# A fourth weight buffer and later products in an attention and SwiGLU kernel

## The chip, the cores and the metric

The kernel runs on one core of a Trainium2 chip. The core has five engines that work side by side, each through its own queue of instructions in order: TensorE (PE in the profile, its weight loads apart as PEld), VectorE (DVE), ScalarE (ACT), GpSimd (POOL) and SyncE (SP, which here only issues transfers). They wait for each other through semaphores. Transfers between the main memory and the on-chip memory (SBUF) run beside them. Matrix products land in PSUM[...].

The metric is the device time of one execution in microseconds (us), as the median of a few runs.

## The reference

Attention comes first: 8 batches, 8 heads, 576 positions, head size 64. Of each row of scores only the 32 largest count. Its output, with the heads side by side, is the input of a feed-forward block with 4,608 tokens, width 512 and 1,536 inner channels.

```python
scores = scale * np.matmul(q, k.transpose(0, 1, 3, 2))
kth = np.partition(scores, -top_k, axis=-1)[..., -top_k:-top_k + 1]
scores = np.where(scores >= kth, scores, -1000000000.0)
attn = np.exp(scores - np.max(scores, axis=-1, keepdims=True))
attn = attn / (np.sum(attn, axis=-1, keepdims=True) + 1e-09)
x = np.matmul(attn, v)          # then (B,H,S,D) -> (B*S, H*D)
g = x @ w_gate
out = (g * (1.0 / (1.0 + np.exp(-g))) * (x @ w_val)) @ w_out
```

The inputs q, k and v and the output are float32. The three weight matrices arrive as float64.

## The kernel before, in words

**Units.** Attention is cut into units of one batch, 128 query rows (64 in the last tile of a batch) and two heads. The main loop (line 833) goes through them and holds several at once in different stages. For unit n, `scores` makes q times k on PE (line 310, line 296 for the short tile) and ACT copies the result to `sc` (lines 315, 301). `select` finds the 32 largest on DVE, with four rounds of MAX8 (line 330) and three of MATCH_REPLACE8 (line 334) per head. `shift` subtracts on POOL (line 345). `weigh` makes the exponentials on ACT (lines 357 and 362), and leaves their sum in `tot`. `normalize` takes the reciprocal on DVE (lines 373, 374) and scales e on POOL (line 380) or ACT (line 378). `turn` transposes e on PE into `etps` (line 394), and ACT copies it (line 395). `values` multiplies with v on PE (line 428), and ACT copies the product into `xT` (line 444), the transposed input of the feed-forward block.

**Feed-forward.** A block has 256 tokens. The first two are done in halves of 128 tokens and in the plain way by `feed_half` (products with w_gate and w_val, line 488; ACT evacuates them in lines 508 to 515, POOL multiplies in lines 511 and 516) and `out_half` (product with w_out into `o_ps`, line 540). From the third block on, `feed` does the work (lines 572 and 638), with a scheme for the last product that needs sums and differences of parts of w_out. It can start only when all six early jobs (four halves in, two halves out) are issued and all heads of the block are in `xT`.

**Rounding.** The weights arrive as float64, that is as pairs of 32-bit words, and the kernel rounds them to float32 by itself from the two words. They come in 36 pieces of 512 KB: 12 of w_gate, 12 of w_val, in turns of two, then 12 of w_out, one per 128 inner channels. `rounded` handles one: SP loads it into a buffer `w` (line 104), ACT makes three passes over it (lines 112, 114, 115), DVE shifts (line 119), POOL adds and multiplies (lines 120, 121), and line 121 writes the rounded piece to its place in `wg`, `wv` or `wo`. Line 121 is also the last reader of the buffer. Buffers of one tag are reused in turn, so the load of a piece waits until line 121 of the piece that had the buffer before. `weights` steps the pieces through three stages with lags, and counts in `ready` how many have been issued to the end. The later part of `weights` forms the sums and differences of w_out on POOL (lines 169, 177, 181, 185); its first three tiles `t` have the tag of the weight buffers too.

**Who decides the order.** The order on PE, DVE, ACT and POOL is the order in which the Python program issues instructions, since the end of the kernel ties each to the one before it on its engine. SP's order is left to the framework. A product is issued when `piece` finds a job that may go on: `feed_half` and `out_half` ask `sure(n)` before each product, and give the turn back when it says no. `sure` does not wait on the chip. It compares a counter while the program is written, so that a product is placed in PE's queue at a point where the rounding of its piece has already been issued. A credit of time per unit (`share`) limits how many products are put into one unit.

Of the kernel before, what the change touches and what calls it, by code (L numbers as in the profile page):

```python
# [10 lines left out]
FP32 = mybir.dt.float32  # L11
I32 = mybir.dt.int32
# [3 lines left out]
P = 128  # L16
# [5 lines left out]
WP = 256  # L22
# [3 lines left out]
def kernel(  # L26
# [39 lines left out]
    DM, DFF = w_gate.shape  # L66
# [5 lines left out]
    MC = DFF // P  # L72
    MS = MC // 2
# [11 lines left out]
    ffn = ctx.enter_context(tc.tile_pool(name="ffn", bufs=2))  # L85
# [14 lines left out]

    def rounded(src, dst):

        w = ffn.tile([P, 2, WP, 2], I32, tag="w", name="w", bufs=3)
        nc.sync.dma_start(
            w[:].rearrange("p c f t -> p c (f t)"), src.bitcast(I32)
        )
        yield
        low, high = w[:, :, :, 0], w[:, :, :, 1].bitcast(FP32)


        size = conv.tile([P, 2, WP], FP32, tag="size", name="size", bufs=3)
        nc.scalar.activation(size[:], high, AF.Abs, scale=2.0**-112)

        nc.scalar.mul(low, low.bitcast(U32), 2.0**-29)
        nc.scalar.sign(high, high)
        yield

        bits = size[:].bitcast(I32)
        nc.vector.tensor_single_scalar(bits, bits, 3, ALU.logical_shift_left)
        nc.gpsimd.tensor_tensor(bits, bits, low, ALU.add)  # L120
        nc.gpsimd.tensor_tensor(dst, size[:], high, ALU.mult)  # L121

    def weights():


        pieces = []
        for f in range(0, DFF, WP):
            for src, dst in ((w_gate, wg), (w_val, wv)):
                for c in range(0, KC, 2):
                    rows = src[c * P : (c + 2) * P, f : f + WP]  # L130
                    pieces.append((
                        rows.rearrange("(c p) f -> p c f", p=P), dst[:, c : c + 2, f : f + WP]
                    ))
        for c in range(MC):
            pieces.append((
                w_out[c * P : (c + 1) * P].rearrange("p (c f) -> p c f", c=2),
                wo[:, c].rearrange("p (c f) -> p c f", c=2),
            ))
        pieces = [rounded(*p) for p in pieces]
        step = [0] * len(pieces)  # L140

        def upto(i, k):

            while 0 <= i < len(pieces) and step[i] < k:
                next(pieces[i], None)
                step[i] += 1


        lags = (5, 2, 0)
        for n in range(2 * len(pieces) + 4):  # L150
            for k, lag in enumerate(lags):
                if (n - lag) % 2 == 0:
                    upto((n - lag) // 2, len(lags) - k)
            ready[0] = max((n - 5) // 2 + 1, 0)
            early[0] = lambda: upto(n // 2, 2)
            yield
        early[0] = lambda: None


        add, sub = ALU.add, ALU.subtract  # L160
        lo, hi = slice(0, DM // 2), slice(DM // 2, DM)
        room = []
        for _ in range(3):
            t = ffn.tile([P, 4, DM // 2], FP32, tag="w", name="t", bufs=3)
            room += [t[:, 0:2], t[:, 2:4]]
        for m in range(0, MQ, 2):
            mm, nn = slice(m, m + 2), slice(MQ + m, MQ + m + 2)
            t3 = room.pop()
            nc.gpsimd.tensor_tensor(t3, wo[:, nn, hi], wo[:, mm, hi], sub)
            T[7] += [t3[:, i, :] for i in range(2)]  # L170
            yield
        while not plain_done:
            yield
        for m in range(0, MQ, 2):
            mm, nn = slice(m, m + 2), slice(MQ + m, MQ + m + 2)
            t1 = wo[:, mm, hi]
            nc.gpsimd.tensor_tensor(t1, t1, wo[:, mm, lo], sub)
            T[5] += [wo[:, m + i, hi] for i in range(2)]
            yield
            t2 = room.pop()  # L180
            nc.gpsimd.tensor_tensor(t2, wo[:, nn, hi], t1, sub)
            T[6] += [t2[:, i, :] for i in range(2)]
            yield
            t4 = conv.tile([P, 2, DM // 2], FP32, tag="size", name="t4", bufs=3)
            nc.gpsimd.tensor_tensor(t4[:], wo[:, nn, lo], t2, sub)
            T[4] += [t4[:, i, :] for i in range(2)]
            yield
        T[1] += [wo[:, m, lo] for m in range(MQ)]
        T[2] += [wo[:, MQ + m, lo] for m in range(MQ)]
        T[3] += [wo[:, MQ + m, hi] for m in range(MQ)]  # L190
        yield

    ready = [0]
    early = [lambda: None]
    plain_done = []
    T = {i: [] for i in range(1, 8)}
    weight = weights()

    def rounding(n):
# [7 lines left out]

    def sure(n):

        return ready[0] >= min(n + 1, 4 * MS + MC)  # L210

    pairs = [(b, hp) for b in range(B) for hp in range(NHP)]
    raw, preps = {}, {}
# [259 lines left out]
    def feed_half(kb, t):  # L473
# [7 lines left out]
        def product(w, g, then):  # L481
            ps = ps_f.tile([P, 4, P], FP32, tag="f", name="f")
            for i in range(4):
                m = 4 * g + i
                while not sure(4 * (m // 2) + (2 if w is wg else 4)):
                    yield None
                for kc in range(KC):
                    nc.tensor.matmul(  # L488
                        ps[:, i, :],
                        w[:, kc, m * P : (m + 1) * P],  # L490
                        x[:, kc, cols],
                        start=(kc == 0),
                        stop=(kc == KC - 1),
                    )
                if i == 3:
                    on_act.append(lambda: then(ps))
                if i % 2 == 1:
                    yield 1
# [25 lines left out]
    def out_half(t):  # L524
# [7 lines left out]
        while not sure(4 * MS + 2):  # L532
            yield None
# [3 lines left out]
        for m in range(MC):  # L537
            while not sure(4 * MS + m + 1):
                yield None
            nc.tensor.matmul(  # L540
                ps[:], hs[m // 4][:, m % 4, :], wo[:, m, :], start=(m == 0), stop=(m == MC - 1)
            )
            if m == MC - 1:

                def finish():
                    nc.scalar.copy(o[:, t, :], ps[:])
                    store(o[:, t, :], t * P)

                on_act.append(finish)
                told.append(t)  # L550
                if t == 1:
                    plain_done.append(True)
            if m % 2 == 1:
                yield 1
# [389 lines left out]
```

## Time and profile before

| | |
|---|---|
| median of 3 runs | 1777.67 us (1777.34 to 1779.84) |
| the profiled execution, its own time | 1777.1 us |
| its span, first to last instruction | 1775.3 us |
| PE busy | 1683.9 us, 95% of the span |
| PEld busy (beside PE) | 1404.2 us, 79% |
| DVE busy | 1484.1 us, 84% |
| ACT busy | 1257.0 us, 71% |
| POOL busy | 798.9 us, 45% |
| granted TensorE clock, mean | 0.970 of full speed |
| loads of weight pieces, issue to landing, median | 3.5 to 3.7 us |
| moved by transfers | 59.73 MB, mean 34 GB/s |

The shares are means over stages that differ. The first feed-forward product starts at 86 us, the last weight piece is rounded at 197 us, the third block of tokens begins at 347 us, and attention's last transposes come at 1709 us; after them only feed-forward work is left. So the profile is read by stage. In a timeline each row gives the start, the length, the engine, the line of the kernel, the operation and, in brackets, the time for which the engine had been idle just before and what released it.

### The profile page before, as it was taken

The page shows a single profiled execution, that of the slowest core. Times are in us where ns is not written, and L with a number is a line of the kernel's source. Part 1 is how long each engine was busy: PE and PEld are TensorE (multiplying, and loading weights), DVE is VectorE, ACT ScalarE, POOL GpSimd, SP SyncE. Part 2 cuts the span into 40 slices and gives each one's busy share as a digit, 9 for nine tenths or more (in the row PEclk, how much of TensorE's full clock was granted, in tenths as well). Part 3 has the DMA queues.
Part 4 walks back from the last instruction along what each step waited for, and adds up shares of the span by engine and source line. Part 5 has one row for each costly group of instructions (what it writes and reads, how often), then busy time and mean ns, then how long its engine had stood idle before and what let it go on. Part 6 is the DMA issues. An engine that isn't in the chain of part 4 may idle for free.

```text
span 1775.3 us, 31791 instructions
## 1 busy us (share of the span) xinstructions
PE 1683.9 (95%) x11396; PEld 1404.2 (79%) x11396; DVE 1484.1 (84%) x3371; ACT 1257.0 (71%) x2869; POOL 798.9 (45%) x910
## 2 busy tenths in 40 slices
PE   4578999799999999999999999999999999999999
PEld 3477588688888878887888878888888888888887
DVE  6999699998898898997989978998988889898300
ACT  7788686777777677767777776767776777676531
POOL 4788545234353525352444425453335343535344
PEclk7689899899999999999999999999999999999999
DMA  7433030002100030001200021000300010000000
GB/s 197 127 106 96 20 81 9 12 2 58 39 1 13 2 81 15 13 1 35 62 13 1 13 60 37 1 13 2 94 1 13 1 44 27 13 1 13 1 13 12
DMA packets 109310, 59.73 MB, mean 34 GB/s; under 512 B 88544, under 2 KB 96992, under 8 KB 109152
## 3 DMA queue, kind: packets, MB, share of 16 engines
q1 hardware_dynamic: 108016, 57.37, 12.2%
q8 instruction: 90, 1.47, 0.4%
q14 instruction: 68, 0.56, 0.1%
q10 hardware_dynamic: 1136, 0.33, 0.1%
HBM read 48.23 MB, written 9.44 MB: 32 GB/s over the span
## 4 chain that ended last, share of the span: by engine, by line
PE 83%; ACT 7%; POOL 4%; DVE 4%; issue 2%; DMA 1%; SPq 0%; POOLq 0%; ACTq 0%
PE f L572 37%; PE av L428 10%; PE x_ps L638 9%; PE s L310 7%; PE y_ps L638 7%; PE etps L394 6%; PE f L488 3%; ACT e L362 2%; PE s L296 2%; DVE e L334 2%; DVE m L330 2%; PE kqps L265 1%; ACT e L357 1%; POOL wo L121 1%; POOL e L380 1%
## 5 line engine op out<-in xcount | busy, mean ns | idle before, releaser
L330 DVE MAX8 m<-e 128x8 f32<-128x576 f32 x864 | 615.5, 749 | 3.3
L334 DVE MATCH_REPLACE8 e<-m,e 128x576 f32<-128x576 f32 x576 | 424.1, 743 | 0.0
L572 PE MATMUL f<-xT,wg 128*128 128x256 f32 x1536 | 353.5, 381 | 0.0
L572 PE MATMUL f<-xT,wv 128*128 128x256 f32 x1536 | 353.1, 380 | 0.0
L572 PEld LDWEIGHTS f<-xT,wg 128*128 128x128 f32 x1536 | 286.8, 190 | 44.4 <-issue 7.9
L572 PEld LDWEIGHTS f<-xT,wv 128*128 128x128 f32 x1536 | 287.1, 190 | 43.4 <-issue 6.8
L608 POOL TENSOR_TENSOR h<-h,half_g 128x512 f32<-128x512 f32 x96 | 122.5, 1276 | 332.9 <-ACT h L607 324.9
L362 ACT ACTIVATE e<-e,bias 128x576 f32<-128x576 f32 x288 | 221.1, 775 | 34.6 <-POOL bias L345 31.5
L394 PE MATMUL etps<-ident,e 128*128 128x128 f32 (+1 forms) x1312 | 182.8, 281 | 42.9 <-POOL e L380 18.4
L357 ACT ACTIVATE e<-sc,m 128x576 f32<-128x576 f32 x288 | 211.2, 785 | 2.6 <-DVE m L330 2.6
L394 PEld LDWEIGHTS etps<-ident,e 128*128 128x128 f32 (+1 forms) x1312 | 154.7, 143 | 72.9 <-POOL e L380 23.4
L334 DVE MATCH_REPLACE8 e<-m,sc 128x576 f32<-128x576 f32 x288 | 212.0, 743 | 0.0
L330 DVE MAX8 m<-sc 128x8 f32<-128x576 f32 x288 | 203.4, 743 | 9.1 <-ACT sc L315 9.1
L613 POOL TENSOR_TENSOR h<-h,val 128x512 f32<-128x512 f32 x96 | 122.5, 1276 | 194.7 <-ACT val L612 170.9
L373 DVE TENSOR_SCALAR tot<-tot 128x1 f32<-128x1 f32 x288 | 37.2, 146 | 199.7 <-ACT e L362 199.6
L315 ACT ACTIVATE sc<-s 128x288 f32<-128x288 f32 x512 | 167.4, 414 | 49.4 <-PE s L310 49.0
L310 PE MATMUL s<-kqT 64*128 64x288 f32 x1024 | 173.3, 450 | 24.5 <-ACT et L395 11.1
L380 POOL TENSOR_TENSOR e<-e,tot 128x576 f32<-128x576 f32 x140 | 161.1, 1155 | 77.0 <-DVE tot L374 69.2
L395 ACT COPY et<-etps 128x512 f32<-128x512 f32 (+1 forms) x448 | 183.4, 489 | 13.5 <-PE etps L394 13.3
L428 PE MATMUL av<-et,v 128*64 128x128 f32 (+1 forms) x2560 | 161.4, 270 | 0.0
L310 PEld LDWEIGHTS s<-kqT 64*128 64x128 f32 x1024 | 96.0, 194 | 71.9 <-issue 22.9
L378 ACT ACTIVATE e<-e,tot 128x576 f32<-128x576 f32 x148 | 118.4, 800 | 42.8 <-DVE tot L374 42.6
(82 smaller groups left out, 2274.5 us busy)
## 6 DMA issues: line engine op xcount, KB each, us to landing
v<-in_v_dram SPq DMA_DIRECT2D x32, 256.0 KB, 3.1
kq_in<-in_k_dram SPq DMA_DIRECT2D x63, 128.0 KB, 2.8
kq_in<-in_q_dram SPq DMA_DIRECT2D x63, 128.0 KB, 3.1
w<-in_moe_w_gate_dram SPq DMA_DIRECT2D x12, 512.0 KB, 3.7
w<-in_moe_w_val_dram SPq DMA_DIRECT2D x12, 512.0 KB, 3.7
w<-in_moe_w_out_dram SPq DMA_DIRECT2D x12, 512.0 KB, 3.5
out_dram<-o SPq DMA_DIRECT2D x38, 128.0 KB, 2.4
out_dram<-o SPq DMA_DIRECT2D x16, 256.0 KB, 2.6
```

The lines of the kernel that those rows point to most:

```text
L310: nc.tensor.matmul(ps[:, 0:half], slab[d, q0 : q0 + P], slab[d, k0 : k0 + half])
L315: nc.scalar.mul(sc[:, i * half : (i + 1) * half], ps[:, 0:half], scale)
L330: nc.vector.max(m[:, t, 8 * r : 8 * r + 8], cur[:, hs])
L334: nc.vector.match_replace(e[:, hs], m[:, t, 8 * r : 8 * r + 8], cur[:, hs], LOWEST)
L357: nc.scalar.activation(e[:, hs], sc[:, hs], AF.Prelu, bias=m[:, t, TOP_K - 1 : TOP_K], scale=-1.0, alpha=SMALL,)
L362: nc.scalar.activation(e[:, hs], e[:, hs], AF.Exp, bias=bias[:, t : t + 1], scale=-1.0 / SMALL, accum_out=tot[:, t : t + 1],)
L380: nc.gpsimd.tensor_tensor(e[:, hs], e[:, hs], tot[:, t : t + 1].to_broadcast([P, S]), ALU.mult)
L394: nc.tensor.transpose(ps[0:kl, c * P : (c + 1) * P], e[:, k0 : k0 + kl], ident[:])
L395: nc.scalar.copy(et[0:kl, c0 : c0 + cn, :], ps[0:kl, 0 : cn * P].rearrange("p (c j) -> p c j", c=cn),)
L428: nc.tensor.matmul(av[d, i, 0:ql], weights_, moving, start=c == (0 if last else J), stop=c == (J if last else J - 1),)
L572: nc.tensor.matmul(ps[:, i, :], w[:, kc, m * P : (m + 1) * P], x[:, kc, :], start=(kc == 0), stop=(kc == KC - 1),)
L638: nc.tensor.matmul(ps, lhsT, T[i][m], start=m == 0, stop=m == MQ - 1)
```

## The change

Three places are edited. The weight buffers `w` (and the tiles `t` with the same tag) get four buffers in place of three; each is 4 KB per partition. And `sure(n)`, which lets the early products go on, asks for three rounded pieces beyond the n needed ones in place of one; the bound at the total of 36 pieces is kept (4 * MS + MC = 36).

```diff
     def rounded(src, dst):
 
-        w = ffn.tile([P, 2, WP, 2], I32, tag="w", name="w", bufs=3)
+        w = ffn.tile([P, 2, WP, 2], I32, tag="w", name="w", bufs=4)
         nc.sync.dma_start(
             w[:].rearrange("p c f t -> p c (f t)"), src.bitcast(I32)
         )
...
         for _ in range(3):
-            t = ffn.tile([P, 4, DM // 2], FP32, tag="w", name="t", bufs=3)
+            t = ffn.tile([P, 4, DM // 2], FP32, tag="w", name="t", bufs=4)
             room += [t[:, 0:2], t[:, 2:4]]
...
     def sure(n):
 
-        return ready[0] >= min(n + 1, 4 * MS + MC)
+        return ready[0] >= min(n + 3, 4 * MS + MC)
```

## The prediction

> **What bounds the kernel now.** I began with the page (TensorE busy 95%, VectorE 84%), then cut the span into stretches. Columns: stretch in us, its length, busy time and instruction count of PE, PEld, DVE, ACT and POOL, granted TensorE clock, DMA share, GB/s.
>
> ```profile
> 133.00:178.00 45.00, 38.58 (x339) 33.68 (x336) 41.68 (x91) 38.53 (x85) 37.60 (x34) 0.97 0.31 97
> 178.00:222.00 44.00, 40.44 (x217) 23.12 (x216) 30.54 (x71) 26.98 (x59) 23.02 (x21) 0.88 0.06 20
> 222.00:311.00 89.00, 87.56 (x795) 78.18 (x795) 84.65 (x190) 67.00 (x159) 42.95 (x50) 1.00 0.18 45
> 311.00:347.00 36.00, 25.82 (x177) 19.72 (x174) 33.75 (x80) 25.72 (x64) 7.30 (x10) 0.81 0.04 15
> 347.00:1600.00 1253.00, 1241.23 (x8391) 1041.13 (x8390) 1120.62 (x2556) 918.28 (x2119) 518.75 (x620) 1.00 0.09 23
> ```
>
> From 347 us on PE is busy 1241.2 of 1253 us and sets the pace. Before, nothing is full: in 178-222 DVE works 30.5 of 44 us, and in 311-347 PE has idle time while DVE works 33.8 of 36. The second fact matters most: just before the steady stage PE waits for attention, whose chain runs through DVE. So time won on DVE before 347 brings the steady stage forward; time won on PE alone does not.
>
> Next the timeline of DVE, gaps in brackets (time, length, engine, line, then idle time before it and its releaser).
>
> ```profile
> 156.06 0.15 DVE L373 TENSOR_SCALAR tot<-tot 128x1 f32<-128x1 f32 x1 [1.47 <-ACT e L362]
> ...
> 182.29 0.15 DVE L373 TENSOR_SCALAR tot<-tot 128x1 f32<-128x1 f32 x1 [2.69 <-ACT e L362]
> ...
> 199.96 0.15 DVE L373 TENSOR_SCALAR tot<-tot 128x1 f32<-128x1 f32 x1 [4.96 <-ACT e L362]
> ```
>
> Between 36 and 347 us DVE waits 24.5 us in all (the waits give 23.8 for `tot` on the exponentials L362, 0.7 for a shift L119). Place by place, most have a second gap of 0.60 behind them, because the second head's exponential is only then ready: 1.50 at 104, 1.25 at 116, 0.57 at 141, 2.07 at 156, 0.58 at 168, 3.29 at 182, 0.68 at 191.7, 5.56 at 200, 3.54 at 221, and 5.2 in six gaps after 222. Who held up the exponentials? ACT's timeline:
>
> ```profile
> 152.12 0.68 ACT L112 ACTIVATE size<-w 128x512 f32<-128x512 f32 x1 [3.77 <-DMA w<-in_moe_w_out_dram]
> ...
> 178.39 0.67 ACT L112 ACTIVATE size<-w 128x512 f32<-128x512 f32 x1 [3.10 <-DMA w<-in_moe_w_out_dram]
> ...
> 190.97 0.66 ACT L112 ACTIVATE size<-w 128x512 f32<-128x512 f32 x1 [6.36 <-DMA w<-in_moe_w_out_dram]
> ...
> 197.46 0.37 ACT L444 COPY xT<-av 128x256 f32<-128x256 f32 x1 [2.31 <-PE av L428]
> ```
>
> Three of the four are L112, a weight piece that has not landed; L357/L362 stand behind it in ACT's order. The waits of ACT give 24.1 us for such landings between 50 and 222 (15.4 for `w_out`, 7.7 for `w_val`, 1.0 for `w_gate`). The fourth waits for PE, so PE's timeline:
>
> ```profile
> 178.34 7.19 PE L540 MATMUL o_ps<-wo,h 128*128 128x512 f32 x12
> 187.50 1.13 PE L540 MATMUL o_ps<-wo,h 128*128 128x512 f32 x2 [1.97 <-POOL wo L121]
> 190.11 2.08 PE L540 MATMUL o_ps<-wo,h 128*128 128x512 f32 x2 [1.49 <-POOL wo L121]
> 192.12 2.29 PE L310 MATMUL s<-kqT 64*128 64x288 f32 x8
> ```
>
> Products o_ps of channels 8 and 9 wait for rounded pieces of `w_out`, and the scores stand behind them: they leave at 192.12 instead of about 187. Why was the piece late? POOL's timeline:
>
> ```profile
> 183.56 1.27 POOL L516 TENSOR_TENSOR h<-h,val 128x512 f32<-128x512 f32 x1 [6.25 <-ACT val L515]
> 184.80 1.28 POOL L120 TENSOR_TENSOR size<-size,w 128x512 int32<-128x512 int32 x1
> ```
>
> POOL has piece 8 of `w_out` next, its ACT part long done (170.6-172.3), but h L516 stands first and waits 6.25 us for `val`, which ACT makes only after the late landing of 178.39.
>
> [...] SP's queue waits 53.3 us on wo L121, 44.6 on wv and 38.5 on wg before it may issue L104. [...] L119 takes 0.41 us in most of its 36 runs and up to 1.46 while POOL is at work. [...] o_ps takes 7.19 us for 12 at 178 (clock 0.75 in 178-192) and 5.32 at 203.
>
> **The change, part by part.** The order of instructions on DVE is unchanged throughout. On PE it differs from 106.8 to 318.7 us of before; then every product has been issued and the rows are the same to the end. So the whole result is by how much attention arrives earlier there. `sure` is asked while the program is written, so it leaves no wait behind, only another order.
>
> *Fourth buffer.* A piece's load may start when the piece four back is rounded, not three: one L121 earlier, which is 2.6 to 13 us of POOL's timeline. A load takes 3.6 us to land. Take piece 10 of `w_out`: issued after L121 of piece 7 (ends 174.8), landed 178.4, ACT waits 3.10. With four buffers it follows piece 6 (ends 169.3), lands at 173, and ACT comes for it at 175.3: no wait. Piece 11 would land near 178 and not 191. The same holds at 100.48 (3.23) and 152.12 (3.77). On SP some w loads now stand ahead of v and kq loads of the first 50 us; v of the fourth pair is needed at 81 us, kq of the next batch at 226, so I cost that at nothing; uncovered it would be one load, 3 us. The 2.55 us gap of DVE at 34 stays: SP's queue is unchanged that far. Tiles of that tag reused as `t` (L164, L169) add no operation.
>
> *Products later.* No matmul is added or removed. At 107 us one block of eight wg matmuls (16 records in the trace, 1.9 us) moves behind the scores. Of o_ps, channels 8 and 9 leave the queue ahead of the scores at 192, and one block of wg moves in. The work issued stays within 0.8-1.3 us of before at each pair of units, so PE has nothing to catch up. On POOL pieces 8 and 9 now stand before h L516, and piece 2 before L380, so rounding waits less for `val`. Newly queued behind a later product is its own h L511/L516, with m3 behind those at 146 us; the products are done by then by my replay (PE at 144), cost 0 to 2 us on POOL, hidden by its gap of 2.9 us at 141.
>
> *Replay of DVE's gaps.* 104: ACT's 3.23 go, gap 1.50 goes. 116: scores 1.9 us earlier on PE; bias L345 on POOL then comes last, gain 0.6. 141: ACT's 1.60 at 131 go, gain 0.3. 156: ACT's 3.77 go, then bias and exponentials are ready 2 us before DVE; gain 1.8. So 4.2 us by 168. 182: ACT is 3.1 earlier, DVE finds the first exponential ready; gain 3.2. 191.7: piece 11 is there, 0.7. At 200 PE comes last: the second etps is released by POOL e L380, itself 4.2 earlier, so it ends at 174.3 and not 178.5; then channels 0 to 7 are 16 instructions of 0.60 us at the low clock (9.6) or 0.44 at full clock (7.1), so the scores leave at 181.4 to 183.9 and not 192.12: 8.2 to 10.7 us earlier. From there to 214.8 PE's queue is the same 22.7 us, some 1 us less where it ran the scores and values at the low clock (2.29 against 1.19 for 8 scores). The gap at 221 is PE's too and stays. After 222 PE is busy 98%, its work equal, so the lead is kept, and at 311-347 DVE carries it on. Sum: 4.2 of the gaps before 168, 5.3 more where PE comes last, 1.0 of clock: 10.5 us (8.2 to 12).
>
> The profiled span becomes 1764.8 of 1775.3, its own time 1766.6 of 1777.1. The median of the runs, 1777.67, lies 0.6 above that one: 1767.2.
>
> Two costs are not shown by the trace. Shifts L119 meet POOL at other moments: 13 of 36 are long now, 10.5 us over 0.41 in all (25.25 - 36 x 0.41); I take no change, with -4 and +5 as ends. [...]
>
> **Rivals.** *Part only* (0.15): the scores are not freed, since etps still waits for e L380 as now, and only 104 to 182 count: 4.2 to 7 us, 1771-1773. For it: L380 holds PE for 17.9 us between 36 and 222. Against: L380 stands behind the same rounding that moves up. *All gaps to 222 go* (0.10): 19 us, 1758.5. Against: PE works 40.4 of 44 us in 178-222, some 35 at the durations of the 1.00 stretches, and cannot fold more than 9 there. *It comes to nothing* (0.10): PE is so full in 178-311 that it merely waits less and VectorE's gaps move to later scores; 1775-1779. Against: PE's idle 10 us at 311-347 show that attention, not PE, decides the arrival. *Slower* (0.08): POOL, with fewer gaps, is at work whenever a shift comes. A collision costs 1.0 us; 23 shifts are still short. Beyond 10 more the gain is gone, beyond 14 it is slower by 0.2%; 20 give 1777.7 - 10.5 + 20 = 1787. Against: shifts stand at fixed places of DVE's order, and POOL's rounding still follows each. That the buffer does nothing is excluded by the 24.1 us of landings on ACT.
>
> **Numbers.** The forecast has 0.57. About 0.2% (3.5 us) is what a measurement of this kernel tells from no change. Faster: forecast, part and all gaps, 0.82; same 0.10; slower 0.08. The range runs from all gaps (1758.5) to the good end of nothing (1775) and leaves out the slower rival and half of the nothing, with 0.03 below: 1758 to 1775. The forecast's own range is 1763 to 1771.
>
> **What would show it.** ACT's waits for w landings between 50 and 222 fall from 24.1 us to under 4; DVE's busy time in the 44 us after 178 rises above 34; no o_ps waits for wo L121; first L572, now at 346.8, starts near 336; from there to the end as long as before (1428.5 us). Wrong if L572 starts near 346, if L119 exceeds 30 us in sum (25.2 now), or if the steady stage changes its length.

## The result, and the profile after

The kernel after takes 1765.38 us (1765.32 to 1765.85) against 1777.51 us (1777.33 to 1779.84) of the kernel before: 12.1 us less, ratio 0.9929 with a 95% interval of 0.9912 to 0.9947. The forecast was 1767.2. The profiled execution took 1765.43 us, its span 1763.6.

The stretches of the kernel after, with the same bounds and columns as those of before:

```profile
133.00:178.00 45.00, 39.76 (x301) 35.53 (x302) 41.13 (x92) 39.37 (x87) 39.08 (x34) 0.85 0.27 85
178.00:222.00 44.00, 43.90 (x306) 28.07 (x304) 37.30 (x83) 28.92 (x66) 23.97 (x24) 0.99 0.10 26
222.00:311.00 89.00, 86.46 (x745) 77.30 (x744) 83.78 (x192) 66.44 (x158) 39.55 (x47) 1.00 0.15 36
311.00:347.00 36.00, 28.69 (x197) 22.70 (x196) 35.86 (x85) 26.93 (x66) 7.88 (x10) 0.86 0.04 16
347.00:1600.00 1253.00, 1241.29 (x8399) 1041.73 (x8398) 1120.43 (x2559) 920.26 (x2125) 523.64 (x628) 1.00 0.09 23
```

VectorE's busy time in 178-222 rises from 30.5 to 37.3 us and PE's from 40.4 to 43.9; the granted clock there is 0.99 and not 0.88. The stretches are cut at the same times, so each holds somewhat later work than before. From 347 us on the busy times and the clock are the same.

The order of VectorE's instructions is the same in both kernels, so the lead (by how much an instruction comes earlier than in the kernel before) can be read instruction by instruction. I took the reciprocal L374 of each unit. It comes 2.8 us earlier at 105 us of before, still 2.7 at 129, 4.0 at 141, 6.6 at 157, only 3.9 at 168, then 5.4 at 183, 10.4 at 201, 10.4 at 222 and 11.2 at 314, and stays at 11.2 until the steady stage begins. The gaps of VectorE that remain between 140 and 222 us are these, without a second one of 0.6 us behind each (timeline, the brackets are idle time and releaser):

```profile
149.49 0.15 DVE L373 TENSOR_SCALAR tot<-tot 128x1 f32<-128x1 f32 x1 [0.53 <-ACT e L362]
...
163.49 0.15 DVE L373 TENSOR_SCALAR tot<-tot 128x1 f32<-128x1 f32 x1 [1.99 <-ACT e L362]
...
189.61 0.15 DVE L373 TENSOR_SCALAR tot<-tot 128x1 f32<-128x1 f32 x1 [1.67 <-ACT e L362]
...
210.54 0.15 DVE L373 TENSOR_SCALAR tot<-tot 128x1 f32<-128x1 f32 x1 [2.94 <-ACT e L362]
```

The gaps at 104, 116, 141 and 182 of before are gone, the one at 200 shrank from 4.96 to 1.67, the one at 221 is the same 2.94. But the gap at 163.49 is new in this size. ScalarE's waits from 50 to 222 us (total, times, longest):

```profile
ACT xT L444 <- PE av L428: 9.8, 7, 2.0
ACT sc L315 <- PE s L310: 4.4, 1, 4.4
...
ACT size L112 <- DMA w<-in_moe_w_gate_dram: 1.9, 1, 1.9
```

Late landings cost 1.9 us where they cost 24.1. ScalarE now waits for TensorE instead: 22.1 us in all, where it was 10.0. Here are TensorE's timeline and then GpSimd's, where the scores had stood behind channels 8 and 9:

```profile
174.47 9.09 PE L540 MATMUL o_ps<-wo,h 128*128 128x512 f32 x16
183.49 1.24 PE L310 MATMUL s<-kqT 64*128 64x288 f32 x8
```

```profile
173.41 1.29 POOL L120 TENSOR_TENSOR size<-size,w 128x512 int32<-128x512 int32 x1
...
176.09 1.27 POOL L120 TENSOR_TENSOR size<-size,w 128x512 int32<-128x512 int32 x1
...
178.77 1.27 POOL L516 TENSOR_TENSOR h<-h,val 128x512 f32<-128x512 f32 x1
```

All o_ps ahead of the scores run without a wait, and the scores leave at 183.49 (192.12 before). Pieces 8 and 9 of w_out are rounded at 173-179, ahead of h L516; before, that multiplication stood first and held them until 184.8 and 187.4. The steady stage starts with TensorE's first product of the third block, the first L572. It comes 11.45 us earlier (346.79 before):

```profile
335.34 3.72 PE L572 MATMUL f<-xT,wg 128*128 128x256 f32 x16
```

From there to the end it is 1428.26 us, against 1428.51 before. In sum, then, all but a quarter of a microsecond of the change of the span was won before 347. But that sum hides two differences that cancel. Up to TensorE's last wait for attention (1709.20 before, 1696.03 after) the steady stage is 1.7 us shorter in the kernel after, and behind that wait the end is 1.5 us longer. The last section shows where such amounts vary from one profile to the next.

The arrival varies too. Three profiles further down have the same instructions up to this point (the repeated kernel after, the one with extra VectorE work late, and the one with an edit at the end). Their first L572 comes at 333.09 to 333.20, 2.2 us earlier still than the 335.34 here. One profile therefore gives the arrival only to about 2 us.

### The profile page after: what moved, and what is told of

Same layout as the page of the kernel before. It is cut to its first block, busy times and chain, and to the rows that moved or that the text cites. A ratio compares the mean times of both kernels' runs of the same rounds, so it can differ in the third digit from the quotient of the medians.

```text
span 1763.6 us, 31788 instructions
## 1 busy us (share of the span) xinstructions
PE 1679.7 (95%) x11396; PEld 1403.7 (80%) x11396; DVE 1483.0 (84%) x3371; ACT 1256.7 (71%) x2869; POOL 797.1 (45%) x910
## 4 chain that ended last, share of the span: by engine, by line
PE 84%; DVE 6%; ACT 6%; POOL 2%; issue 1%; SPq 1%; DMA 0%; ACTq 0%; POOLq 0%
PE f L572 37%; PE av L428 9%; PE x_ps L638 9%; PE s L310 7%; PE y_ps L638 7%; PE etps L394 7%; PE f L488 4%; DVE m L330 3%; DVE e L334 3%; ACT e L362 2%; PE s L296 2%; PE kqps L265 1%; ACT e L357 1%; DVE size L119 1%; ACT sc L315 1%
## 5 line engine op out<-in xcount | busy, mean ns | idle before, releaser
L572 PE MATMUL f<-xT,wg 128*128 128x256 f32 x1536 | 354.4, 381 | 0.0
L572 PE MATMUL f<-xT,wv 128*128 128x256 f32 x1536 | 353.1, 380 | 0.0
L572 PEld LDWEIGHTS f<-xT,wg 128*128 128x128 f32 x1536 | 287.5, 190 | 44.7 <-issue 7.9
L572 PEld LDWEIGHTS f<-xT,wv 128*128 128x128 f32 x1536 | 287.1, 190 | 43.4 <-issue 6.8
L315 ACT ACTIVATE sc<-s 128x288 f32<-128x288 f32 x512 | 167.1, 413 | 54.7 <-PE s L310 54.2
L373 DVE TENSOR_SCALAR tot<-tot 128x1 f32<-128x1 f32 x288 | 36.6, 145 | 187.6 <-ACT e L362 187.4
L395 ACT COPY et<-etps 128x512 f32<-128x512 f32 (+1 forms) x448 | 182.9, 488 | 13.8 <-PE etps L394 13.6
```

The lines of the kernel that those rows point to most:

```text
L315: nc.scalar.mul(sc[:, i * half : (i + 1) * half], ps[:, 0:half], scale)
L395: nc.scalar.copy(et[0:kl, c0 : c0 + cn, :], ps[0:kl, 0 : cn * P].rearrange("p (c j) -> p c j", c=cn),)
L572: nc.tensor.matmul(ps[:, i, :], w[:, kc, m * P : (m + 1) * P], x[:, kc, :], start=(kc == 0), stop=(kc == KC - 1),)
```

## The experiments

**The two halves of the change.** PE, DVE, ACT and POOL have the order of before in the first kernel, and that of after in the second, so each half stands alone.

```diff
-        w = ffn.tile([P, 2, WP, 2], I32, tag="w", name="w", bufs=3)
+        w = ffn.tile([P, 2, WP, 2], I32, tag="w", name="w", bufs=4)
```

(and the same for `t`; sure stays at n + 1)

> Four weight buffers, products placed as in the kernel before (sure asks for n + 1). PE, DVE, ACT and POOL have the order of the kernel before, only the loads on SP move. Theory landing: the late landings on ACT were what held DVE, so this alone gives 8 to 11 us (about 1767 to 1769.5), ACT's waits for w landings between 50 and 222 us fall from 24.1 to under 4, and the first L572 starts near 337. Theory order: it is the place of the products behind or ahead of the scores that counts, so this gives 4 us or less (1773.5 or more), and the gap of DVE at 200 us stays at about 5.

Measured: 1768.34 us against 1778.83, ratio 0.9938 (0.9925 to 0.9952). Landings on ScalarE between 50 and 222 fall to 2.8 us. The gain of 10.5 us fits the landing theory in size, and its ratio can't be told from that of the whole change (0.9929, 0.9912 to 0.9947). But the profiled execution, the slowest of this kernel (1772.69), has its first L572 at 339.43, a lead of 7.4 us only, and the gap of VectorE at 193 is still 3.65. Its end is long too, 1431.5 us from the first L572 on against 1428.3 in the kernel after, so how early an execution near the median arrives is not known. TensorE shows why a gap is left:

```profile
183.03 1.13 PE L540 MATMUL o_ps<-wo,h 128*128 128x512 f32 x2 [1.12 <-POOL wo L121]
185.66 1.12 PE L540 MATMUL o_ps<-wo,h 128*128 128x512 f32 x2 [1.50 <-POOL wo L121]
186.72 1.24 PE L310 MATMUL s<-kqT 64*128 64x288 f32 x8
```

The products still stand ahead of the scores and still wait for pieces 8 and 9, which GpSimd rounds behind h L516. They are earlier because `val` is earlier (the multiplication starts at 179.09 and not at 183.56).

```diff
-        return ready[0] >= min(n + 1, 4 * MS + MC)
+        return ready[0] >= min(n + 3, 4 * MS + MC)
```

(with three buffers)

> Three weight buffers, products placed as in the kernel after (sure asks for n + 3). PE, DVE, ACT and POOL have the order of the kernel after. Theory landing: gain of 1 to 4 us (1773.5 to 1776.5), ACT still waits 12 us or more for landings between 50 and 222. Theory order: gain of 8 us or more (1769.5 or less). If the two parts add up without touching each other, this gain and that of the buffers alone sum to 12.1 us.

Measured: 1772.01 us, ratio 0.9958 (0.9945 to 0.9970), about 7 us faster. Neither theory had the gain right (1 to 4, or 8 and more). The landings still hold ScalarE, as its waits show:

```profile
ACT size L112 <- DMA w<-in_moe_w_val_dram: 7.1, 4, 3.4
ACT size L112 <- DMA w<-in_moe_w_out_dram: 6.9, 4, 3.2
...
ACT size L112 <- DMA w<-in_moe_w_gate_dram: 4.5, 2, 3.8
```

That is 18.5 us in sum where it was 24.1, and yet VectorE's gap at 200 us has gone altogether. The scores follow the products without a stop:

```profile
178.90 8.73 PE L540 MATMUL o_ps<-wo,h 128*128 128x512 f32 x16
187.55 1.24 PE L310 MATMUL s<-kqT 64*128 64x288 f32 x8
```

The first L572 is at 339.44, the same lead of 7.4 us as with the buffers. Together the two leads would be 14.7 us; the kernel after has 11.45. So in these profiles 3.3 us are won by either half alone, and most of that can be placed at the scores of 192 us. The buffers bring these forward by 5.4 us (to 186.72), the order by 4.6 (187.55), both by 8.6 (183.49): 1.3 us in common. And each half alone, like both, runs TensorE's queue from there to the next unit's scores in 21.0 us and not in 22.7: 1.7 us more in common.

The size of this overlap is less sure than that it exists. With the arrivals of 333.1 to 333.2 in place of 335.34 it would be about 1 us. By the medians it is 5 us (10.5 and 6.8 alone, 12.1 together). The times alone don't show that the later products add anything to the buffers; the scores at 183.49 and not at 186.72 speak for it.

**Another distance.** Two more kernels have four buffers, with n + 2 and with n + 4 in `sure`.

> Four buffers, sure asks for n + 2. Only PE's order differs from the kernel after (31 lines of the listing), the other four queues are the same. Theory landing: within 1.5 us of the kernel after (1764 to 1767). Theory order: 2 us or more slower than the kernel after, since some products stand ahead of scores again.

> Four buffers, sure asks for n + 4. Products go still later, and the order of PE differs from the kernel after far beyond the early stage. Theory landing: no gain from more distance, 1764 to 1768. Theory order: another 1 to 3 us faster (1762 to 1764). If the early products no longer all fit before the third block starts, slower: up to 1775.

n + 2: 1767.32 us, ratio 0.9932 (0.9919 to 0.9944), not to be told from the kernel after, with its first L572 at 335.02. n + 4: 1761.92 us, 0.9914 (0.9899 to 0.9929), which looks better by 3 us; but its times lay in two groups, near 1761.9 and 1767.4, and its profile (of the second group) leads at the first L572 by 12.0 us, hardly more than the 11.45 of after. So it was run again beside the kernel after.

> The kernel after unchanged, as the ground for the other three of this set: ratio to the kernel before 0.992 to 0.994.

> Four buffers with n + 4 again, beside the kernel after on one chip. Theory distance (one more piece of distance helps by itself): 2 to 5 us faster than the kernel after, as the medians of different chips had it. Rival (that difference was the clock at the end of some runs): within 1.5 us of the kernel after.

The kernel after: 1765.88 us, 0.9927 (0.9915 to 0.9940). n + 4: 1765.15 us, 0.9916 (0.9901 to 0.9930), between 1761.65 and 1765.87. The medians differ by 0.7 us on one chip, and the two profiles arrive together (first L572 at 333.13 and 333.14). A gain of one or two us is not excluded, but no gain from the distance is shown. n + 3 is no sharp choice.

**Who sets the pace?** Four kernels give one engine extra work, in the early stage or in the steady one, on the kernel after. The extra maxima go to a tile that nobody reads, and the repeated products overwrite themselves with the same values.

```diff
-        dve(2, beside=False)
+        dve(2, beside=False); [nc.vector.max(spare[:], state[n]["sc"][:, 0:S]) for _ in range(2) if 2 <= n < 10]
```

(early; late is once in each of units 80 to 89)

> The kernel after, with two extra MAX8 (into a spare tile, read by nobody) in each of units 2 to 9: 16 instructions at 0.67 us from one to the next, 10.6 us of VectorE time before about 140 us. Theory arrival (before 347 us attention's chain through DVE sets the pace and time won or lost there moves everything after it): 8 to 11 us slower than the kernel after, so about 0.9985 to 1.0005 of the kernel before, first L572 8 to 11 us later, and the time from there to the end unchanged. Rival (TensorE sets the pace there): 3 us slower or less.

> The kernel after, with one extra MAX8 in each of units 80 to 89: 6.7 us of VectorE time in the steady stage. Theory (TensorE sets the pace there, VectorE has 10% idle): within 2 us of the kernel after, ratio to the kernel before 0.992 to 0.994. Rival (VectorE sets the pace there as well): 5 to 7 us slower than the kernel after.

```diff
-                    nc.tensor.matmul(
+                    [nc.tensor.matmul(
                         ps[:, 0:half], slab[d, q0 : q0 + P], slab[d, k0 : k0 + half]
-                    )
+                    ) for _ in range(2 if 4 <= n < 12 else 1)]
```

(early; late is units 80 to 87)

> The kernel after, with the score products of units 4 to 11 written twice into the same bank: 32 more matmuls (64 records), 1.2 us of TensorE per unit at full clock, 9.4 us in all, before about 140 us. Theory arrival: TensorE has idle time there and the extra work only delays scores a little: 0 to 4 us slower than the kernel after. Rival (TensorE sets the pace there): 8 us slower or more.

> The kernel after, with the score products of units 80 to 87 written twice: the same 9.4 us of TensorE work in the steady stage. Theory (TensorE sets the pace there): 8 to 10 us slower than the kernel after, all of it between the first L572 and the end. Rival: less than 4 us.

| kernel | median, us | ratio to before (95%) | against after, 0.9929 |
|---|---|---|---|
| VectorE early, +10.6 us of work | 1775.60 | 0.9985 (0.9978 to 0.9992) | 10 us slower |
| VectorE late, +6.7 us | 1766.04 | 0.9931 (0.9915 to 0.9948) | same |
| TensorE early, +9.4 us | 1765.51 | 0.9931 (0.9916 to 0.9946) | same |
| TensorE late, +9.4 us | 1773.82 | 0.9973 (0.9965 to 0.9982) | 8 us slower |

Each pair splits as the theory of arrival has it. With VectorE's extra work early the first L572 comes at 344.18, 8.8 us later than in the kernel after (11 us later than in the three profiles of the same order), and with TensorE's extra work late it is not later:

```profile
344.18 3.72 PE L572 MATMUL f<-xT,wg 128*128 128x256 f32 x16
```

```profile
334.79 3.72 PE L572 MATMUL f<-xT,wg 128*128 128x256 f32 x16
```

In the second the loss lies behind that point, which is 1437.3 us from the end of the span; in the other kernels that keep the order of the kernel after from there it is 1428.3 to 1431.0. So up to about 145 us, where both early tests end, time on VectorE counts almost in full and that on TensorE not measurably; in the steady stage it is the reverse. The stretch between was not tested. There TensorE is busy 43.9 of 44 us (178-222) and 86.5 of 89 (222-311) in the kernel after, and the half that only moves its products (and the copies behind them) won 7.4 us, so time on TensorE may well count there too.

**The end.** Several profiles showed one more place. TensorE waits near the end for ScalarE's e, with nothing to do, and then its clock is low for some time (0.51 from 1697.5 to 1701.0 us in the kernel after). This is the second of the last two groups of transposes and the first products of the last block in the run with VectorE's early work:

```profile
1704.94 0.77 PE L394 MATMUL etps<-ident,e 128*128 128x128 f32 x5 [2.61 <-ACT e L378]
...
1708.26 5.98 PE L572 MATMUL f<-xT,wg 128*128 128x256 f32 x16
1714.08 3.62 PE L572 MATMUL f<-xT,wv 128*128 128x256 f32 x16
```

16 records of wg take 5.98 us, and the 16 of wv behind them 3.62; the granted clock in the 5.9 us from 1708.3 was 0.61. The edit keeps some products of the block before for that place:

```diff
-            credit[0] = 8.0
+            credit[0] = 8.0 if n < NU - 1 else 3.0
```

> The kernel after with one edit at the end of the main loop: the credit for products is 3 and not 8 in the last unit, so that products of the last but one block stand between the last two groups of transposes. In the profiles so far TensorE waits 2.6 us there for ACT's e, and in some of them its clock then falls to about half for 3 to 6 us. Theory end: 2 to 5 us faster than the kernel after (0.9895 to 0.992 of before). Rival (the work only changes places, the end is set by the last block): within 1 us of the kernel after.

> n + 4 and the edit at the end together. If both theories hold: 4 to 9 us faster than the kernel after (0.9875 to 0.9905 of before). If only the one at the end: as the kernel named tail.

With the edit alone the same place reads

```profile
1688.69 1.56 PE L638 MATMUL x_ps<-wo,h 128*128 128x256 f32 x6
1690.09 0.71 PE L394 MATMUL etps<-ident,e 128*128 128x128 f32 x5
1690.64 1.46 PE L638 MATMUL x_ps<-wo,h 128*128 128x256 f32 x6
...
1693.78 3.72 PE L572 MATMUL f<-xT,wg 128*128 128x256 f32 x16
```

and the wait and the slow products have both gone. 1759.32 us (1759.19 to 1759.60), ratio 0.9892 (0.9878 to 0.9905): 6.6 us faster than the kernel after on the same chip, more than I had expected, and 18 us faster than the kernel before. From the first L572 to the end it takes 1424.3 us, against 1430.0 in the kernel after of the same set; both profiles arrive at 333.1. Of these 5.7 us, 2.6 are the wait, and the rest is the slow stretch: 0.7 ahead of the first wg products of the last block, 2.3 from there to the end. With n + 4 as well it is 1762.13 us, 0.9903 (0.9890 to 0.9917): not more than the edit alone, and not the sum. The fastest version here is the change with the edit at the end.

## Why the prediction was right

*The frame held where it was tested.* It said that DVE decides before 347 and PE after it, from idle shares. The four runs with extra work show it up to about 145 us and in the steady stage. That time won on PE alone does not bring the steady stage forward goes too far: from 168 to 201 us the lead grows from 3.9 to 10.4, and 4.9 of that came at 200, where the prediction's own replay had PE last. The first L572 came at 335.3 where about 336 was said. No o_ps waits for wo L121, and DVE's busy time in the 44 us after 178 is 37.3 us, both as said. The time behind 347 is the same in sum, as said; that it agrees to 0.25 us, by two differences that cancel, is luck. So is part of the close hit: the lead at 222 was 10.4 where 10.5 was said, and the three other profiles of the same order have 12.5 to 12.6 there, beyond the upper end of 12.

*Fourth buffer.* Right in kind: ScalarE's waits for landings between 50 and 222 us went from 24.1 to 1.9, and the gap at 182 (3.29 with its second part) went whole. In size it fell short: the replay adds to 7.4 us by 183, where the kernel after has 5.4, and the buffers alone 4.5.

*Scores at 192.* The replay had them at 181.4 to 183.9 and they left at 183.49 (181.21 to 181.34 in the three other profiles). From there to the scores of the next unit TensorE needed 21.0 us and not 22.7; the 1.0 set for the clock (0.50 from 192.12 to 194.40 in the kernel before) should have been 1.7. At 221 the gap stayed, as said.

*Shifts.* I took no change; the sum of L119 is 25.0 us where it was 25.2, with 12 long ones and not 13 (26.8 to 27.7 us in the three other profiles). The slower rival needed over ten more long ones. But they moved: the shift at 99.5 runs 0.42 and not 1.31, those at 113 and 114.8 run 0.92 and 1.48 and not 0.42 and 0.41. This is why the lead at 105 was 2.8 and not 1.5, and why nothing was added at 116, where 0.6 was said and the gap of 1.25 did go. At 182 the gap of 3.29 went but only 1.6 were won, since two shifts there ran 1.31 and 1.41 instead of 0.41. Place by place the shifts blur the replay; in sum they count for little.

*Where a step was wrong.* "PE has nothing to catch up" and "the products are done by then by my replay (PE at 144)" failed at 156 to 168. The sum of products is nearly that of before, but in this pair of units they stand in one row of four groups ahead of the scores, and they began later than I had them. TensorE stood 2.87 us at 135 until the score copies L315 had freed a place in PSUM, and then ran at a lower clock (0.85 in 133-178, not 0.97). The chain of the kernel after, in order of time:

```profile
149.92 5.81 PE f L488 x52
155.73 1.17 PE s L310 x8
156.90 2.36 PE av L428 x40
```

Products until 155.7, then scores, values, and behind them ScalarE's exponential, for which VectorE waits 1.99 and 0.61 us at 163, where it had waited 0.58. With a shift that now ran 1.00 and not 0.42 that took back 2.7 of the 6.6 us won by then. I had 4.2 by 168 and it was 3.9: right in sum, and by luck: a gain that I had too small (the gap at 156 and two shifts) and a loss that I had not. Some 1.4 to 1.7 us of the loss return in the three other profiles. The rest came from slow products in this one, from 136 to 144 us (clock 0.68). They are slow again at 172 to 183 (0.70), where the repeated kernel after needs less for the transposes and for these 16 products, which took 9.09 us above:

```profile
172.63 8.72 PE L540 MATMUL o_ps<-wo,h 128*128 128x512 f32 x16
```

Together this is how the repeated kernel comes to a lead of 12.6 us at 201.

*Which half does it.* The prediction told the buffers as the main part up to 182 and the order as the part at 192. The profiles show each half worth about 7.4 us of arrival, and a part in common that the prediction did not have: it did not say what one half would do without the other. The rival "part only" falls, since the scores were freed. "All gaps to 222 go" falls as well: gaps of 6.0 us are left between 140 and 200, and 3.5 at 210. What I had left at nothing behind 222 gave 0.9 in sum: the gap at 313 shrank from 2.11 to 0.85, and smaller changes at 268 to 291 took back a part.

## What to carry to other kernels

Find where the stage that sets the end begins, and ask which engine decides that moment. Until that moment, time on an engine with slack is not worth winning. But the engine that decides can change on the way, so test each stretch with a little extra work. A product that may have to wait for data, in a queue kept in order, delays all that stands behind it (here the scores, behind waits of 1.97 and 1.49 us): place it behind the work that the pace setter needs. A buffer and an order that free the same wait can share a part of their gain, so measure each alone before adding them up. And repeat a profile before reading a single microsecond from it.

## What was not expected of the hardware

After the wait of 2.61 us of TensorE near the end, the first 16 records of wg took 3.72 us in the profile of the kernel before, 4.63 in that of after, and 5.98 in the run shown above, at a clock of 0.61. From the first L572 to the end it was 1428.3 to 1431.5 us in kernels that have the same order there. The clock behind the wait was 1.00 in the kernel before (1709.2 to 1717.0 us) and 0.51 in the kernel after (1697.5 to 1701.0). So the same wait is followed by a slow stretch of different length from one profile to the next, or by none. What decides it was not shown.

The steady stage has such places too. In both kernels TensorE waits 1.84 us for ScalarE's copy of the transposes (L395), before at 832.14 and after at 819.03. These are the same 16 products behind that wait, first in the kernel before (clock 1.00), then in the one after (0.50):

```profile
834.11 1.04 PE L428 MATMUL av<-et,v 128*64 128x128 f32 x16
```

```profile
821.58 1.92 PE L428 MATMUL av<-et,v 128*64 128x128 f32 x16
```

Here VectorE's lead falls from 13.1 to 11.5 us. At two other such waits (2.33 and 1.84 us), at 625 and 1038 us of before, it is the kernel before that runs slowly (clock 0.50 in 626-629 and 1039-1042, and 1.00 behind both waits in the kernel after), and the lead grows by 1.6 each time. This is how two differences came to cancel in the result.

With the wait near the end filled there is no slow stretch at that place in either of the two profiles that have the edit (3.72 us in both). The four times of the edit alone lie within 0.4 us of each other. With n + 4 as well, though, one lies at 1758.96 and three at 1762.04 to 1762.34, so the groups of times of n + 4 do not come from the end alone. The places in the steady stage are worth 1.6 us each and may be the cause. It was not shown, since no trace of an execution of the faster group was kept.
